# A rarely taken branch in a routed-expert kernel: its DMAs on GpSimd, its skipping arm next to the branch, no prefetch marks

## The chip, the cores and the metric

One core of one Trainium2 chip runs the whole program. The metric is device microseconds of one execution; the kernel before takes 772.91 us (median of three). TensorE (PE in the profile) multiplies matrices, VectorE (DVE), ScalarE (ACT) and GpSimd (POOL) do the rest of the arithmetic, SyncE (SP) issues most DMAs. Each engine runs its own instruction stream and waits on semaphores for the others.

## The reference, cut to what matters

Three layers follow each other: attention within clusters, a mixture of 8 experts in which each token goes to one expert, and a bilinear layer.

```python
# x: (1536, 512), the rows of the attention's output
expert_idx = np.argmax(xn @ en.T / tau, axis=1)      # xn, en: normalised rows
gate_w = probs[np.arange(N), expert_idx]
for e in range(8):
    mask = expert_idx == e                           # how many rows: known at run time
    h = np.maximum(x[mask] @ w1[e], 0.0)             # w1[e]: (512, 1024)
    out[mask] = gate_w[mask, None] * (h @ w2[e])     # w2[e]: (1024, 512)
return ((out @ w_a) * (out @ w_b) @ w_out)           # w_a, w_b: (512, 1536)
```

How many tokens an expert gets is not known when the program is built.

## The kernel before, in words

Up to about 289 us the attention runs, and near its end each token's row is scattered by GpSimd into `xs_d` in DRAM, where every expert has a stretch of its own (L739). Then the experts take their turns in order of their size. `WIDTHS` (L26) gives each turn a fixed number of rows, 256 to 160, which the program computes whether or not the expert has so many. A loop over G (L1433) steps through 8 turns of 8 slices of the hidden layer; slice G's first product is in `layer1(G)`, its second two steps later in `layer2(G - LAG)`, and at the end of a turn `ys_e` holds the results, which `put_rows` (L1305) writes to `ys_d` by a DMA of SyncE.

An expert with more rows than its turn's width is "crowded". `limits()` (L1059) computes on VectorE the largest surplus, `most`. At G == 5 (`GR`) `rare()` (L1172) is called: every engine loads `most` into a register (L1174) and branches (L1175). Where it is above zero, the body computes the surplus rows of each expert in a loop of 128 rows at a time, with the expert's weights loaded anew. For the inputs that are timed `most` is zero, so every engine skips the body; the loops in it do not run. A skipping arm of its own stands for the body in each engine's stream: it adds to every semaphore what the body would have added, so that later waits find the same counts. Before it adds to a semaphore it waits until all that was counted on it earlier has arrived. A DMA that SyncE issues counts on one of eight rings' semaphores, which it shares with ScalarE's DMAs; DMAs that GpSimd issues count on eight others.

Weights come by SyncE. The experts' weights of most turns are loaded into four `raw` buffers of 512 KB (`load_raw`, L156) and split by ScalarE (L207) and VectorE (L208) into a high and a low part in the tiles `w`; a raw buffer is free again when VectorE has read it. The turns of widths 160 and 176 take theirs unsplit, by `load_whole` (L180), which at G == 5 issues four loads right behind the branch. `load_xe` (L1134) loads a turn's rows from `xs_d` by a DMA of ScalarE's queue into one of two buffers, which it shares with the tiles `ys_e`; so the third turn's load waits until `ys_0` has been written out, and what stands behind it in ScalarE's stream waits with it. The order of all this is written out by hand: each engine works through its stream in program order.

Before the change three engines have a mark for the branch (`mark_branch_hint_location`), which names the arm that is likely and becomes a prefetch instruction in that engine's stream: TensorE (L1173), VectorE (L1453) and SyncE (L1488).

Of the kernel before, what the change touches and what calls it, by code (L numbers as in the profile page):

```python
# [22 lines left out]
P = 128  # L23
# [8 lines left out]
GR = 5  # L32
# [16 lines left out]
def kernel(  # L49
# [15 lines left out]
    nc = tc.nc  # L65
# [5 lines left out]
    NTOK = B * S  # L71
# [10 lines left out]
    RX = NTOK + P  # L82
# [14 lines left out]
    xs_d = dram.tile([NE * RX, DM], F32, name="xs_d")  # L97
    ys_d = dram.tile([DM, NTOK + CAP], F32, name="ys_d")
    ys_v = ys_d.rearrange("(j p) n -> p j n", p=P)
# [3 lines left out]
    chunks = []  # L103
# [78 lines left out]
    def skip_whole():  # L182
        while nsplit[0] // 4 in whole:
            nsplit[0] += 4
            ndone[0] += 4
# [671 lines left out]
    for s in range(nst):  # L857
        g_, h, t = steps[s]
        pp = g_[0]
        i = s % SPP  # L860
# [206 lines left out]
    def further():  # L1067

        nc.vector.tensor_tensor(out=prod, in0=col(turn_c), in1=row(turn_c), op=ALU.is_gt)
        summed(obase, prod, row(over))  # L1070
        summed(turn_of, at, row(turn_c))
        nc.vector.tensor_tensor(out=bef, in0=col(turn_of), in1=row(turn_of), op=ALU.is_gt)
        summed(pbase, bef, row(held))
        nc.vector.tensor_reduce(out=key[:, 0, 0:1], in_=over.rearrange("p o e -> p (o e)"), axis=AX.X, op=ALU.add)
        nc.vector.tensor_tensor(out=pbase, in0=pbase, in1=key[:, :, 0:1].to_broadcast([P, 1, NE]), op=ALU.add)
        nc.vector.tensor_copy(ov_i[:, :NE], obase[0:1, 0, :])
        nc.vector.tensor_tensor(out=prod[0:1], in0=at[0:1].rearrange("p e q -> p q e"), in1=pbase[0:1].to_broadcast([1, NE, NE]), op=ALU.mult)
        with nc.allow_low_precision(reason="whole numbers below 2^24"):
            nc.vector.tensor_reduce(out=ov_i[:, NE:2 * NE], in_=prod[0:1], axis=AX.X, op=ALU.add)
            nc.vector.tensor_tensor(out=ov_s, in0=over[0:1].rearrange("p o e -> p e o").to_broadcast([1, NE, OVM]),  # L1080
                                    in1=ovt.rearrange("p (o j) -> p o j", o=1).to_broadcast([1, NE, OVM]), op=ALU.is_gt)
            nc.vector.tensor_reduce(out=ov_i[:, 2 * NE:3 * NE], in_=ov_s, axis=AX.X, op=ALU.add)
            nc.vector.tensor_tensor(out=ov_i[:, 3 * NE:], in0=ebase[0:1, 0, :], in1=cap[0:1, 0, :], op=ALU.add)
        nc.vector.tensor_copy(cnt_i, cnt[0:1, :, 0])
# [85 lines left out]


    def rare():  # L1172
        tc.mark_branch_hint_location("rare", "LikelyTaken", engines=[mybir.EngineType.PE])  # L1173
        n_most = nc.values_load(most, min_val=0, max_val=NTOK)  # L1174
        with tc.If(n_most > 0, label="rare"):  # L1175
            further()
            ovw = [big.tile([P, 2, 4, 512], F32, tag=f"w{NSLOT - 1 - c}", name=f"ov_w{c}") for c in range(2)]
            ovb_ = big.tile([P, 8, 512], F32, tag=f"w{NSLOT - 3}", name="ov_b")
            xr, yr = ovb_[:, 0, :], ovb_[:, 1, :]
            xrT = ovb_[:, 2, :].rearrange("p (j t) -> p j t", t=P)  # L1180
            hT = ovb_[:, 3:5, :].rearrange("p a (j t) -> p (a j) t", t=P)

            ph = ps_s.tile([P, 4, P], F32, tag=f"sc{CT}", name="ov_ph")
            py = ps_s.tile([P, DM], F32, tag=f"sc{CT + 1}", name="ov_py")
            pt = py.rearrange("p (j t) -> p j t", t=P)
            nc.vector.memset(yr, 0.0)
            n_t = [nc.values_load(cnt_i[0:1, e:e + 1], min_val=0, max_val=NTOK) for e in range(NE)]
            for e in range(NE):
                i = nc.sync.dma_start(out=xs_d[bass.ds(n_t[e] + e * RX, P), :], in_=yr)
                if e == 0:  # L1190
                    for o in scatters:
                        tc.add_manual_dep(i.ins, o.name, DATA, reason="rows of every scatter")
            for e in range(NE):
                n_e = nc.values_load(ov_i[0:1, 2 * NE + e:2 * NE + e + 1], min_val=0, max_val=OVM)
                row = nc.values_load(ov_i[0:1, e:e + 1], min_val=0, max_val=NTOK)
                first = nc.values_load(ov_i[0:1, 3 * NE + e:3 * NE + e + 1], min_val=e * RX, max_val=e * RX + CAP)
                with tc.For_i(0, n_e, 1) as it:
                    nc.sync.dma_start(out=xr, in_=xs_d[bass.ds(nc.s_assert_within(first + it * P, min_val=e * RX, max_val=e * RX + NTOK), P), :])
                    for c in range(FF // 512):
                        for z in range(2):  # L1200
                            nc.sync.dma_start(out=ovw[c][:, z], in_=chunks[4 * e + 2 * c + z])
                    for j in range(DC):
                        nc.tensor.transpose(pt[:, j, :], xr[:, j * P:(j + 1) * P], ident)
                    nc.vector.tensor_copy(xrT, pt)
                    for c in range(FF // 512):
                        for f in range(4):
                            for j in range(DC):
                                nc.tensor.matmul(ph[:, f, :], ovw[c][:, 0, j, f * P:(f + 1) * P], xrT[:, j, :], start=(j == 0), stop=(j == DC - 1))
                        nc.vector.tensor_scalar(out=hT[:, 4 * c:4 * c + 4, :], in0=ph, scalar1=0.0, scalar2=None, op0=ALU.max)
                    for c in range(FF // 512):  # L1210
                        for f in range(4):
                            for j in range(DC):
                                nc.tensor.matmul(pt[:, j, :], ovw[c][:, 1, f, j * P:(j + 1) * P], hT[:, 4 * c + f, :],
                                                 start=(c == 0 and f == 0 and j == 0), stop=(c == FF // 512 - 1 and f == 3 and j == DC - 1))
                    nc.vector.tensor_copy(yr, py)
                    nc.sync.dma_start(out=ys_v[:, :, bass.ds(nc.s_assert_within(row + it * P, min_val=0, max_val=NTOK), P)],
                                      in_=yr.rearrange("p (j t) -> p j t", t=P))


# [119 lines left out]
    def split_x2(ck, u):  # L1339

        hi, lo = xT_t["b", ck, u]
        nc.scalar.copy(hi, lo.bitcast(F32))
        nc.vector.tensor_sub(lo, lo.bitcast(F32), hi)
# [89 lines left out]
    for G in range(total_f + tot + LAG):  # L1433
        I = G - total_f

        skip_whole()
        room = 4 * (NSLOT + 2 * (max(G - LAG, 0) // 4)) - nsplit[0]
        if 4 * NCE <= nsplit[0] and I < 0 and G % NF > 1:
            narrow_a(min(room, 1))
        if G == 1:  # L1440
            ranks()
        if G == 2:
            limits()
        if G == GR:
            rare()
        if I < 0:
            layer1(G)
            if G in (2, NF - 1):
                load_xe(1 if G == 2 else 2)
            if G == NF:  # L1450
                further()
            if G == GR - 2:
                tc.mark_branch_hint_location("rare", "LikelyTaken", engines=[mybir.EngineType.DVE])  # L1453
            e, f = divmod(G, NF)
            if 2 * NF <= G < 3 * NF:
                next(rr, None)
            if G > 3 * NF:
                next(gg, None)
            if f == (5 if e else NF - 2):
                if e + 1 < NE:  # L1460
                    trans_x(e + 1, xe_t[e + 1])
            if f == 5 and 0 < e < NE - 2:
                load_xe(e + 2)
        elif I < tot:
            bil1(I)
            next(pg_, None)
        for ck, u in X2S.get(I, ()):
            split_x2(ck, u)
        if I >= LAG:
            for J in after[I]:  # L1470
                bil2(J)
        elif G >= LAG:
            layer2(G - LAG)
        for ck, u in X2.get(I, ()):
            load_x2(ck, u)
        put_rows(G - LAG)
        if 3 <= G < total_f:
            load_whole(G)
        if nsplit[0] < 4 * NCE:

            ramp = RAMP0 + 2 * min(G, GR - 2) + RAMP * max(G - GR + 1, 0)
            split_some(min(room, 2 * G + lead - nsplit[0], ramp - nsplit[0], 4 * NCE - nsplit[0]))
        elif I < 0:
            narrow_c()
            narrow_b(1)
            narrow_d()
        if G == GR - 1:
            tc.mark_branch_hint_location("rare", "LikelyTaken", engines=[mybir.EngineType.SP])  # L1488


# [28 lines left out]
```

## Time and profile before

| | us |
|---|---|
| median of three runs | 772.91 |
| lowest and highest | 771.47, 772.96 |
| the profiled execution's own time | 772.48 |
| its span, first to last instruction | 770.4 |
| TensorE busy | 749.1 |
| VectorE, ScalarE, GpSimd busy | 465.4, 374.2, 106.0 |

The span is what the profile shows; the own time is what the measurement of the same execution gives, and 2.1 us lie around the span. A busy time is a mean over stages: the branch lies at 300 to 317 us, at the start of the expert layer. In the views "engine name with q" is that engine's queue of instructions (register loads, branches, semaphores, DMA issues), which do not count as busy.

### The profile page before, as it was taken

How to read it: one execution, taken by the hardware profiler on the slowest of the kernel's cores; microseconds unless marked ns; L12 is line 12 of the kernel's file. 1: busy time of each engine (PE TensorE's matmuls, PEld its weight loads, DVE VectorE, ACT ScalarE, POOL GpSimd, SP SyncE). 2: the span in 40 equal slices, each digit the busy share in tenths (PEclk: the TensorE clock that was granted, in tenths of full speed). 3: DMA queues.
4: the chain of work that ended last, by engine and by line, in shares of the span. 5: the costliest groups of instructions: out<-in, count | busy, mean ns of one | idle time of the engine just before them, and what ended most of it. 6: DMA issues, size and time to landing. Idle time of an engine off the chain costs nothing.

```text
span 770.4 us, 12666 instructions
## 1 busy us (share of the span) xinstructions
PE 749.1 (97%) x4777; PEld 629.4 (82%) x4777; DVE 465.4 (60%) x911; ACT 374.2 (49%) x769; POOL 106.0 (14%) x145
## 2 busy tenths in 40 slices
PE   8989999999999998999999999999999999999996
PEld 5667777767777668999999999888898888888996
DVE  7877676787767666477876799686653121121211
ACT  5666766678666674366655555344323121111211
POOL 6303203052200040000000003222001020000201
PEclk9999999999999999999999999999999999999999
DMA  6327223163121036789879877464411010000100
GB/s 187 85 85 266 48 76 85 59 199 100 46 48 32 28 110 202 275 310 294 274 235 255 284 229 235 113 138 112 134 29 55 1 55 1 1 0 1 55 1 28
DMA packets 48132, 91.87 MB, mean 119 GB/s; under 512 B 6328, under 2 KB 20280, under 8 KB 48064
## 3 DMA queue, kind: packets, MB, share of 16 engines
q1 hardware_dynamic: 43856, 81.01, 34.9%
q0 software_dynamic: 2304, 6.31, 2.1%
q10 hardware_dynamic: 1904, 3.67, 1.4%
q8 instruction: 39, 0.64, 0.3%
q14 instruction: 29, 0.24, 0.1%
HBM read 69.27 MB, written 14.04 MB: 108 GB/s over the span
## 4 chain that ended last, share of the span: by engine, by line
issue 28%; PE 23%; DMA 4%; DVE 2%; POOL 1%; ACT 1%; SPq 0%; POOLq 0%; ACTq 0%; DVEq 0%
PE ab L1169 7%; PE y L1286 4%; PE y L1290 2%; PE h L1250 2%; DMA raw<-in_moe_w_dram 2%; PE h L1169 2%; PE h L1242 2%; PE o_sc L1414 1%; DMA ys_d<-ys 1%; PE y L1291 1%; PE h L1251 1%; POOL out_dram L1392 1%; DVE w L208 1%; ACT w L207 1%; PE o_pp L1414 1%
## 5 line engine op out<-in xcount | busy, mean ns | idle before, releaser
L1373 DVE TENSOR_TENSOR ga<-ab,ga 128x256 f32<-128x256 f32 (+1 forms) x48 | 26.7, 557 | 156.8 <-PE ab L1169 111.0
L1169 PE MATMUL ab<-xT_b,w 128*128 128x256 f32 (+1 forms) x720 | 113.2, 305 | 0.0
L606 ACT ACTIVATE E<-sc,nmx 128x768 f32<-128x768 f32 x96 | 86.7, 903 | 54.0 <-DVE nmx L601 42.1
L1169 PE MATMUL ab<-x,w 128*128 128x512 f32 x432 | 108.1, 390 | 0.0
L1169 PEld LDWEIGHTS ab<-xT_b,w 128*128 128x128 f32 x720 | 98.6, 190 | 7.2
L601 DVE TENSOR_REDUCE nmx<-sc 128x1 f32<-128x768 f32 x96 | 91.4, 953 | 7.6 <-PE sc L593 6.5
L1169 PEld LDWEIGHTS ab<-x,w 128*128 128x128 f32 x432 | 81.1, 188 | 17.2
L621 PEld LDWEIGHTS et<-ident,E 128*128 128x128 f32 x576 | 62.3, 140 | 34.6 <-ACT ET L625 14.4
L621 PE MATMUL et<-ident,E 128*128 128x128 f32 x576 | 82.3, 279 | 4.2 <-ACT E L606 1.7
L627 DVE COPY ET<-et 128x384 f32<-128x384 f32 x96 | 52.6, 548 | 53.7 <-PE et L621 50.8
L1372 ACT COPY ga<-ab 128x256 f32<-128x256 f32 (+1 forms) x48 | 23.0, 480 | 126.9 <-PE ab L1169 123.8
L592 PE MATMUL sc<-K,Q 80*128 80x512 f32 x192 | 72.9, 380 | 1.4 <-DMA Q<-ohT 1.1
L648 PE MATMUL pv<-ET,v 128*64 128x384 f32 (+2 forms) x408 | 73.0, 479 | 0.6 <-ACT ET L625 0.5
L208 DVE TENSOR_TENSOR w<-raw,w 128x1024 fp32r<-128x1024 f32 x48 | 58.1, 1219 | 21.1 <-ACT w L207 20.5
L1414 PE MATMUL o_sc<-w,g 128*128 128x512 f32 x288 | 69.5, 390 | 0.0
L1374 ACT CAST g<-ga 128x256 fp32r<-128x256 f32 (+1 forms) x48 | 24.7, 514 | 84.1 <-DVE ga L1373 84.1
L1414 PEld LDWEIGHTS o_sc<-w,g 128*128 128x128 f32 x288 | 53.9, 188 | 11.3
L593 PE MATMUL sc<-K,Q 128*128 128x512 f32 x192 | 61.2, 340 | 0.0
L1286 PE MATMUL y<-hh,w 128*128 128x256 f32 (+3 forms) x416 | 59.3, 290 | 0.0
L207 ACT CAST w<-raw 128x1024 fp32r<-128x1024 f32 x48 | 50.3, 1049 | 18.5 <-DMA raw<-in_moe_w_dram 11.7
L1286 PEld LDWEIGHTS y<-hh,w 128*128 128x128 f32 x416 | 54.4, 190 | 0.3 <-DVE ys L1260 0.3
L625 ACT COPY ET<-et 128x384 f32<-128x384 f32 x96 | 45.6, 475 | 2.6 <-PE et L621 2.6
(268 smaller groups left out, 1204.0 us busy)
## 6 DMA issues: line engine op xcount, KB each, us to landing
raw<-in_moe_w_dram SPq DMA_DIRECT2D x48, 512.0 KB
w<-in_moe_w_dram SPq DMA_DIRECT2D x16, 512.0 KB
raw<-in_moe_w_a_dram SPq DMA_DIRECT2D x12, 512.0 KB
raw<-in_moe_w_b_dram SPq DMA_DIRECT2D x12, 512.0 KB
raw<-in_moe_w_out_dram SPq DMA_DIRECT2D x12, 512.0 KB
xs_d<-zero SPq DMA_DIRECT2D x8, 512.0 KB
xe<-xs_d ACTq DMA_DIRECT2D x7, 512.0 KB
v<-in_v_dram SPq DMA_DIRECT2D x8, 384.0 KB
```

The source lines that it names most:

```text
L207: nc.scalar.copy(hi, w)
L208: nc.vector.tensor_sub(lo, w, hi)
L592: nc.tensor.matmul(ps[:, lo:hi], Q3[:, qs], K3[:, h * S + lo:h * S + hi], start=True, stop=False)
L593: nc.tensor.matmul(ps[:, lo:hi], Q2[:, qs], K2[:, h * S + lo:h * S + hi], start=False, stop=True)
L601: nc.vector.tensor_reduce(out=nmx[pp][:, h, t:t + 1], in_=sc[s], axis=AX.X, op=ALU.max, negate=True)
L606: nc.scalar.activation(e, sc.pop(s), AF.Exp, bias=nmx[pp][:, h, t:t + 1], accum_out=sums[pp][:, t, h:h + 1])
L621: nc.tensor.transpose(pt[:, j * P:(j + 1) * P], e[:, kt * P:(kt + 1) * P], ident)
L627: nc.vector.tensor_copy(dst, src)
L648: nc.tensor.matmul(pv[h * D:(h + 1) * D, :], vt[:, h, kt, :], ets[g, h][:, kt, :n * P], start=(kt == 0), stop=(kt == NT - 1))
L1169: nc.tensor.matmul(ps, s_, m_, start=(i == 0), stop=(i == len(ops) - 1))
L1286: nc.tensor.matmul(ys_ps[e][j // 2][:, j % 2, :wd], w[:, m_, ff, j * P:(j + 1) * P], s_, start=(f == 0 and i == 0 and j % 2 == 0), stop=(l ...
L1414: nc.tensor.matmul(o_ps[ck][t], s_[:, t * P:(t + 1) * P], w_[:, m_], start=(f == 0 and i == 0), stop=(J == I and f == NF2 - 1 and i == 2))
```

## The change

The DMAs in the body are issued by GpSimd instead of SyncE; the branch asks that its false arm, which skips, comes next in the stream; the three marks go. The body is otherwise the same, and the timed inputs still skip it.

```diff
     def rare():
-        tc.mark_branch_hint_location("rare", "LikelyTaken", engines=[mybir.EngineType.PE])
         n_most = nc.values_load(most, min_val=0, max_val=NTOK)
-        with tc.If(n_most > 0, label="rare"):
+        with tc.If(n_most > 0, label="rare", preferred_fallthrough_block=False):
             further()
...
             for e in range(NE):
-                i = nc.sync.dma_start(out=xs_d[bass.ds(n_t[e] + e * RX, P), :], in_=yr)
+                i = nc.gpsimd.dma_start(out=xs_d[bass.ds(n_t[e] + e * RX, P), :], in_=yr)
...
                 with tc.For_i(0, n_e, 1) as it:
-                    nc.sync.dma_start(out=xr, in_=xs_d[...])
+                    nc.gpsimd.dma_start(out=xr, in_=xs_d[...])
                     for c in range(FF // 512):
                         for z in range(2):
-                            nc.sync.dma_start(out=ovw[c][:, z], in_=chunks[4 * e + 2 * c + z])
+                            nc.gpsimd.dma_start(out=ovw[c][:, z], in_=chunks[4 * e + 2 * c + z])
...
-                    nc.sync.dma_start(out=ys_v[...],
+                    nc.gpsimd.dma_start(out=ys_v[...],
                                       in_=yr.rearrange("p (j t) -> p j t", t=P))
...
-            if G == GR - 2:
-                tc.mark_branch_hint_location("rare", "LikelyTaken", engines=[mybir.EngineType.DVE])
...
-        if G == GR - 1:
-            tc.mark_branch_hint_location("rare", "LikelyTaken", engines=[mybir.EngineType.SP])
```

## Rows read from the trace of the kernel before

**Rows 1.** The page's engine table: busy us, share of the span, instructions.
```profile
PE 749.1 (97%) x4777; PEld 629.4 (82%) x4777; DVE 465.4 (60%) x911; ACT 374.2 (49%) x769; POOL 106.0 (14%) x145
```

**Rows 2.** TensorE's timeline: start, us, operation, in brackets the idle time before.
```profile
304.55 1.67 PE L1169 MATMUL h<-xT,w 128*128 128x256 f32 x12 [0.30 <-PEq L1175]
...
342.14 1.70 PE L1169 MATMUL h<-xT,w 128*128 128x256 f32 x12 [1.36 <-DVE hh L1247]
...
354.92 1.70 PE L1169 MATMUL h<-xT,w 128*128 128x256 f32 x12 [0.40 <-DVE hh L1247]
...
367.03 0.47 PE L1290 MATMUL y<-hh,w 128*128 128x448 f32 x1 [1.06 <-DVE ys L1299]
```

**Rows 3.** The branch's line: ns (min/median/max), first and last start in us.
```profile
L1175 SPq EVENT_SEMAPHORE  x9: 17/17/17, 311.4 to 316.3; - x9
L1175 PEldq EVENT_SEMAPHORE  x2: 51/51/51, 304.3 to 304.4; - x2
L1175 DVEq EVENT_SEMAPHORE  x2: 21/21/21, 304.5 to 304.6; - x2
L1175 POOLq COMPARE_BRANCH  x1: 53/53/53, 300.2 to 300.2; - x1
L1175 PEldq COMPARE_BRANCH  x1: 397/397/397, 302.6 to 302.6; - x1
...
L1175 DVEq COMPARE_BRANCH  x1: 84/84/84, 303.9 to 303.9; - x1
...
L1175 POOLq EVENT_SEMAPHORE  x1: 17/17/17, 304.6 to 304.6; - x1
L1175 SPq COMPARE_BRANCH  x1: 70/70/70, 307.4 to 307.4; - x1
```

**Rows 4.** Waits of SyncE's queue, 300 to 320 us: total us, times, longest.
```profile
SPq L1175 <- SPq L1175: 8.4, 4, 4.0
```

**Rows 5.** The DMA view, 300 to 320 us in 40 equal slices: rate.
```profile
GB/s 205 168 385 406 430 369 209 352 377 234 66 131 172 234 324 328 344 344 373 397 385 401 393 430 307 250 172 127 78 25 25 12 0 0 4 168 295 266 406 393
```

**Rows 6.** SyncE's timeline behind the branch.
```profile
316.83 2.20 SPq L180 DMA_DIRECT2D w<-in_moe_w_dram  x4
...
320.54 0.42 SPq L1310 DMA_DIRECT2D ys_d<-ys  x1
```

**Rows 7.** The chain that ended last, in order of time: start, us, what.
```profile
320.54 9.47 DMA ys_d<-ys
...
334.52 4.91 DMA raw<-in_moe_w_dram
```

**Rows 8.** ScalarE's timeline behind the branch.
```profile
327.26 1.07 ACT L1159 CAST xT<-xT 128x512 fp32r<-128x512 f32 x2
...
330.61 1.04 ACT L207 CAST w<-raw 128x1024 fp32r<-128x1024 f32 x1 [2.27 <-DMA ys_d<-ys]
```

**Rows 9.** Who waited for whom, GpSimd: total us, times, longest.
```profile
POOL tab_d L994 <- DVE id_gate L987: 113.9, 1, 113.9
```

**Rows 10.** Busy us by window; the last three columns: granted clock, DMA share, GB/s.
```profile
320.00:340.00 20.00, 20.00 (x157) 20.00 (x157) 11.56 (x14) 11.56 (x18) 0.00 (x0) 1.00 0.96 336
```

**Rows 11.** The page's DMA queues that fetch instructions: packets, MB, share of 16 engines.
```profile
q8 instruction: 39, 0.64, 0.3%
q14 instruction: 29, 0.24, 0.1%
```

**Rows 12.** The windows at the end of the span, with the granted clock.
```profile
766.00:768.00 2.00, 0.00 (x0) 0.00 (x0) 0.00 (x0) 0.00 (x0) 0.35 (x2) 0.92 0.43 168
768.00:770.00 2.00, 0.00 (x0) 0.00 (x0) 0.00 (x0) 0.00 (x0) 0.00 (x0) 0.50 0.00 0
```

**Rows 13.** TensorE's timeline at the start and at the end of the span.
```profile
1.21 4.02 PE L263 MATMUL wps<-ones 128*128 128x512 bf16 x9 [1.21 <-DVE ones L247]
...
6.55 0.83 PE L263 MATMUL wps<-ones 128*128 128x512 bf16 x3
...
762.78 1.52 PE L1414 MATMUL o_pv<-w,g 128*128 128x512 f32 x6
```

More of the change, by code (lines that the diff above doesn't have):

```diff
@@ L1197, in rare @@
                 with tc.For_i(0, n_e, 1) as it:
-                    nc.sync.dma_start(out=xr, in_=xs_d[bass.ds(nc.s_assert_within(first + it * P, min_val=e * RX, max_val=e * RX + NTOK), P), :])
+                    nc.gpsimd.dma_start(out=xr, in_=xs_d[bass.ds(nc.s_assert_within(first + it * P, min_val=e * RX, max_val=e * RX + NTOK), P), :])
                     for c in range(FF // 512):
                         for z in range(2):
-                            nc.sync.dma_start(out=ovw[c][:, z], in_=chunks[4 * e + 2 * c + z])
+                            nc.gpsimd.dma_start(out=ovw[c][:, z], in_=chunks[4 * e + 2 * c + z])
                     for j in range(DC):
@@ L1215, in rare @@
                     nc.vector.tensor_copy(yr, py)
-                    nc.sync.dma_start(out=ys_v[:, :, bass.ds(nc.s_assert_within(row + it * P, min_val=0, max_val=NTOK), P)],
+                    nc.gpsimd.dma_start(out=ys_v[:, :, bass.ds(nc.s_assert_within(row + it * P, min_val=0, max_val=NTOK), P)],
                                       in_=yr.rearrange("p (j t) -> p j t", t=P))
```

## The prediction, made before the changed kernel was run

> **What bounds the kernel now.** I read the page first, its table of engines: TensorE is busy 749.1 of 770.4 us [rows 1]. What the change can gain is therefore bounded by TensorE's idle time behind the branch, and what it can lose by any hole that it makes there. So the second view was TensorE's timeline with the idle time ahead of each piece [rows 2]. From the branch to 445 us there are four holes: 0.30 us at the branch itself, then 1.36 us at 342.14, 0.40 us at 354.92 and 1.06 us at 367.03, 3.12 us together and 2.82 without the first. The third view was the two lines of the branch [rows 3], where the reader is to look, engine by engine, at the time from the compare to the first semaphore of the skipping arm: GpSimd 300.2 + 0.05 to 304.6 (4.35 us), SyncE 307.4 + 0.07 to 311.4 (3.9 us), VectorE 303.9 + 0.08 to 304.5 (0.5 us), TensorE 302.6 + 0.4 to 304.3, which is only when its own last matmul had ended. The waits of SyncE's queue give the same line 8.4 us in four waits, the longest 4.0 [rows 4]: the first is the jump, the other three are the arm's semaphores, each waiting until one ring of earlier loads has landed. The DMA view of that stretch shows what this costs [rows 5]: from 313 to 317.5 us (places 27 to 35 of the 40) the rate falls from about 390 to some 50 GB/s, so 4.5 us x 0.34 MB/us = 1.5 MB, three loads of 512 KB, are not moved.
>
> Last SyncE's timeline [rows 6], the chain that ended last [rows 7] and ScalarE's timeline [rows 8]. Behind the arm SyncE issues four weight loads from 316.83 on, a raw load, and at 320.54 the write of `ys_0`, which lands 9.47 us later, behind those five. The next `xe` load needs that tile's buffer and stands in ScalarE's queue ahead of the weight split of L207, which starts at 330.61 after 2.27 us of idling for that write; from there the ring raw load, L207, L208, next raw load runs late and opens the three later holes.
>
> **The change part by part.** *DMAs to GpSimd.* Of SyncE's nine semaphores in the skipping arm the eight of its DMA rings go to GpSimd's arm; SyncE keeps the one of its register loads. SyncE is free some 5 us earlier for this alone (311.4 instead of 316.3). GpSimd's rings last carried the scatters, all issued ahead of its own compare at 300.2, and GpSimd then waits 113.9 us for `id_gate` [rows 9], so nine short semaphores there cost nothing. If that cover were gone they would cost up to the 5 us that SyncE's took. Who waits for them now are the first weight loads and the `xe` load behind the arm; GpSimd has done them before SyncE reaches its compare at 307.4. What then follows: the five loads are issued from 312 or 308 instead of 316.83, while the loads issued earlier are still under way (the last lands at 316.3, when SyncE passes its last semaphore), so the hole in the DMA closes; at the 336 GB/s of the stretch behind [rows 10] one load takes 1.56 us, so the five have landed by 316.3 + 5 x 1.56 = 324.1 and `ys_0`, issued when it is computed (about 320), by 325 at the latest. ScalarE reaches the `xe` load at 328.3 (end of the casts of L1159, 327.26 + 1.07): its 2.27 us are gone, and nothing is late in their place. Carried along the ring this takes back 2.27 of the 2.82 us of later holes; at the most all of it. ScalarE's `xe` load just behind the branch also stops waiting for SyncE; TensorE waits for neither, so that is worth nothing.
>
> *The arm behind the branch, and no marks.* Where things stand now is read from rows 3: the time is lost ahead of the semaphores and none after them (SyncE's last at 316.3, its next DMA at 316.83; TensorE's last at 304.4, its next matmul at 304.55 [rows 2, 6]). So today the body of the rare path lies behind the branch, then the skipping arm, then the rest of the kernel. The flag swaps the two arms. Nothing in the diff moves the rest, which both arms must reach, so I take the order to become: arm, body, rest. Then the skip isn't free of its jump. The jump only stands behind the semaphores instead of ahead of them, and nothing marks it for prefetch any more.
>
> For SyncE and GpSimd that changes little: they paid 3.9 and 4.35 us with the old order (SyncE with a mark) and pay it again; SyncE's loads start at about 312. VectorE, now unmarked, may lose 4 us from 304.6 on; its next work waits for TensorE's matmuls, which come later still: nothing.
>
> TensorE is the one that pays. Its arm can't start its semaphores before its last matmul has ended (304.25), and the jump comes after them, at about 304.55, with an empty array. The body has 8 experts x 68 matmuls, each with a weight load: 1,088 instructions. One queue fetches code in 39 pages of 0.64 MB / 39 = 16 KB [rows 11]; I take it for TensorE's, whose 2 x 4777 matmuls and weight loads [rows 1] are 245 a page, while the other engines have far fewer; the jump is then over 4.4 pages. Its price isn't in the trace: the bounds are 0.5 us (VectorE's, target there) and 5.5 us (GpSimd's 4.35 and one more microsecond for a page twice the size). I take 4.6: GpSimd's and SyncE's mean of 4.1, and 0.5 for the page, since 0.3% of 16 engines' 770 us over 39 pages is 0.95 us each against 0.1% over 29, 0.42 us, for the others [rows 11].
>
> The Trainium skill ("Runtime: NRT & Kernel Launch", section "Instruction fetch mechanics") speaks against the change in the same way: a taken branch to a page outside the two-page window has to fetch it before going on. The 3.9 and 4.35 us of rows 3 agree; by this rule an order without a jump would cost TensorE nothing and the one that I assume would cost it a fetch.
>
> A hole of almost 5 us touches the clock. At the end of the kernel the last matmul ends at 764.30 and the granted clock is at half (1.2 GHz) from 767.7, worked out from 0.92 in 766:768 and 0.50 behind [rows 12, 13]. At the start the nine warming matmuls from 1.21 take 4.02 us, 0.42 us apart, where three later ones fit into 0.83 [rows 13]: at least 4 us at half rate. So a fall would cost 0 (it doesn't come) to 2.6 us; I take 1.5.
>
> **The sum**, against the profiled execution (772.48 us, span 770.4; the median of the three others is 772.91, the lowest 771.47, so it stands in their middle): 772.48 + 4.6 (jump) + 1.5 (clock) - 2.6 (later holes; between 2.27 and 2.82, since the delay gives the loads more lead) = 776.0 us.
>
> **The rivals.** *No jump is left.* If the rest of the kernel lies directly behind the arm and the body is put elsewhere, no engine jumps: SyncE's loads start at 307.6, TensorE keeps its 0.3 us hole (it waits for its own matmuls), and only the gain is left: 772.48 - 2.3 = 770.2, at most 769.3 with 2.82 and the first hole gone. For it: the flag is meant to say what comes next. Against it: today's order has arm and rest side by side with the body in front, and a swap of the two arms is all the diff asks for. The point that decides is TensorE's first matmul behind its semaphores: at 304.6 here, near 309 in the forecast.
>
> *The jump is cheap.* The same order, but TensorE pays 3.5 us or less and the clock stays up, against 2.8 us given back: 773.2. For it: the clock's fall at the end came 3.4 us after the last matmul, close to such a hole. Against: the two engines that jump to code that isn't there pay more with smaller pages.
>
> *Nothing moves.* The DMAs' move does nothing for TensorE because the ring of raw loads sets the later holes by itself, and no jump is left: 772.5. Against: ScalarE's 2.27 us stand in that chain.
>
> **How the numbers follow.** Jump as forecast 0.55 (own range 773.8 to 778); no jump 0.3 (769.3 to 771.2); cheap jump 0.1; nothing moves 0.05. The measurement tells 0.2% (1.5 us) from no change. Slower: 0.53, the forecast but for its lowest end. Faster: 0.29, all but the upper edge of the second. Same: 0.18, the two last and those edges. The range from 769.9 to 777.8 reaches over the other side's case; it leaves out its lowest part and a clock that stays low longer than at the start.
>
> **What would show it.** In the changed profile: SyncE's arm has one semaphore and its queue's waits at L1175 lose the three on rings (if not, the first part is wrong); the DMA rate has no hole at 313 to 317; ScalarE's 2.27 us wait for `ys_0` is gone; TensorE has a hole of 4 to 5.5 us right behind its semaphores, with the granted clock below 1 behind it. A hole of 0.3 us there and 770 us makes the forecast wrong at the step "the rest stays behind the body"; a hole of 4.6 us with the later holes as before makes the gain wrong.

## The result and the profile after

The changed kernel takes 778.09 us (median of five runs, 777.54 to 780.89) against 771.47 us for the kernel before (five runs, 770.31 to 772.96): a ratio of 1.0094, 95% interval 1.0074 to 1.0114 (the two medians alone give 1.0086). It is slower by 0.9%. The forecast was 776.0 us with a range up to 777.8, so the sign and the mechanism came out and the size did not: the time lies 0.3 us above the range, and the change costs some 7 us where 3.5 were forecast.

The profiled execution of the changed kernel took 780.70 us with a span of 779.2 us. First the engine table of its page, and its two queues that fetch instructions [rows 1, 11]:

```profile
PE 751.3 (96%) x4777; PEld 631.4 (81%) x4777; DVE 465.5 (60%) x911; ACT 373.9 (48%) x769; POOL 106.2 (14%) x145
...
q8 instruction: 40, 0.66, 0.4%
q14 instruction: 32, 0.26, 0.1%
```

The same 4777 matmuls are busy for 2.2 us longer, which is already a hint at the clock. The branch's line is L1174 now (one line was removed ahead of it). ns are min/median/max, then the first and the last start; where a group has two, the second COMPARE_BRANCH is the jump at the end of the arm [rows 3]:

```profile
L1174 POOLq EVENT_SEMAPHORE  x5: 17/43/43, 299.8 to 300.1; - x5
...
L1174 PEldq COMPARE_BRANCH  x2: 95/4021/7947, 302.0 to 304.0; - x2
...
L1174 PEldq EVENT_SEMAPHORE  x2: 51/51/51, 303.7 to 303.9; - x2
L1174 SPq COMPARE_BRANCH  x2: 41/47/53, 306.6 to 306.8; - x2
L1174 POOLq INC_SWDGE_SEM  x1: 412/412/412, 300.2 to 300.2; - x1
...
L1174 SPq EVENT_SEMAPHORE  x1: 17/17/17, 306.7 to 306.7; - x1
```

The reader is to see three things. On every engine the semaphores now start right behind the compare (TensorE's once its last product has ended, at 303.7), so the arm does lie behind the branch. Each engine shows two COMPARE_BRANCH where it had one, so a jump is left, behind the arm. TensorE's lasts 7.95 us, from 304.0 to 312.0. SyncE's shows as 0.04 us, but its next instruction starts only at 313.0, of which more further down. SyncE has one semaphore left of nine; GpSimd's take 0.8 us and nobody waits for them.

TensorE's timeline, with the idle time ahead of a piece in brackets [rows 2]:

```profile
302.09 1.60 PE L1285 MATMUL y<-hh,w 128*128 128x256 f32 x12
312.03 2.93 PE L1169 MATMUL h<-xT,w 128*128 128x256 f32 x12 [8.34 <-issue]
314.76 2.60 PE L1285 MATMUL y<-hh,w 128*128 128x256 f32 x12
317.19 1.60 PE L1169 MATMUL h<-xT,w 128*128 128x256 f32 x12
...
348.34 1.70 PE L1169 MATMUL h<-xT,w 128*128 128x256 f32 x12 [0.71 <-DVE hh L1246]
...
375.92 0.47 PE L1289 MATMUL y<-hh,w 128*128 128x448 f32 x1 [1.17 <-DVE ys L1298]
```

and the windows over it (the last three columns are the granted clock, the DMA share and GB/s):

```profile
304.00:306.00 2.00, 0.00 (x0) 0.00 (x0) 0.00 (x0) 0.00 (x0) 0.00 (x0) 1.00 0.67 225
306.00:308.00 2.00, 0.00 (x0) 0.00 (x0) 0.00 (x0) 0.00 (x0) 0.00 (x0) 0.69 1.06 323
308.00:310.00 2.00, 0.00 (x0) 0.00 (x0) 0.00 (x0) 0.00 (x0) 0.00 (x0) 0.50 1.02 358
...
314.00:316.00 2.00, 2.00 (x11) 2.00 (x11) 0.42 (x1) 1.00 (x2) 0.00 (x0) 0.50 0.04 13
316.00:318.00 2.00, 2.00 (x15) 2.00 (x14) 1.23 (x1) 0.31 (x1) 0.00 (x0) 0.75 0.52 189
318.00:320.00 2.00, 2.00 (x21) 2.00 (x20) 0.76 (x2) 0.81 (x2) 0.00 (x0) 1.00 0.98 353
```

From 304 to 312 no engine computes at all. In that hole the granted clock falls to 0.50 (1.2 GHz), and most of the next 24 matmuls run at it, until about 317 (the window 316 to 318 is at 0.75): from 312.03 to 317.19 they take 5.16 us, where the two pieces behind the jump took 2.95 before (the first starts at 304.55, and the third at 307.50 in the same timeline). That is 2.2 us, the same 2.2 by which TensorE's busy time grew.

The bill of the two profiled executions, 779.2 - 770.4 = 8.8 us of span: 8.04 for the jump (8.34 - 0.30), 2.2 for the clock, less 0.94 for the two later holes (0.71 + 1.17 against 2.82), less 0.56 because TensorE reached the branch earlier (303.69 against 304.25). The sum is 8.74. Around the span lie 1.5 us against 2.1, so the own times differ by 8.2. That is no chance: the time around the span is about 1.5 us (1.43 to 1.54) in every execution of every kernel with the body's DMAs on GpSimd, and about 2.1 (2.02 to 2.15) in those of the kernel before.

The five runs of the changed kernel lie at 777.5 to 778.1 and at 780.7 to 780.9; the profiled one belongs to the upper, some 2.6 us above the median.

### The profile page after: what moved, and what is told of

The parts are those of the page before. It is cut to its first block, busy times and chain, and to the rows that moved or that the text cites. A ratio compares the mean times of both kernels' runs of the same rounds, so it can differ in the third digit from the quotient of the medians.

```text
span 779.2 us, 12681 instructions
## 1 busy us (share of the span) xinstructions
PE 751.3 (96%) x4777; PEld 631.4 (81%) x4777; DVE 465.5 (60%) x911; ACT 373.9 (48%) x769; POOL 106.2 (14%) x145
## 4 chain that ended last, share of the span: by engine, by line
issue 29%; PE 24%; DMA 3%; DVE 3%; POOL 1%; ACT 1%; POOLq 0%; SPq 0%; DVEq 0%; ACTq 0%
PE ab L1169 6%; PE y L1285 4%; DMA raw<-in_moe_w_dram 2%; PE y L1289 2%; PE h L1249 2%; PE h L1169 2%; PE h L1241 2%; PE o_sc L1413 1%; DVE w L208 1%; PE y L1290 1%; PE h L1250 1%; POOL out_dram L1391 1%; PE o_pp L1413 1%; PE o_pv L1413 1%; ACT w L207 1%
## 5 line engine op out<-in xcount | busy, mean ns | idle before, releaser
L1169 PE MATMUL h<-xT,w 128*128 128x256 f32 (+1 forms) x288 | 40.0, 289 | 11.0 <-issue 8.3
```

Of the source, the lines that this page charges most:

```text
L1169: nc.tensor.matmul(ps, s_, m_, start=(i == 0), stop=(i == len(ops) - 1))
```

## The experiments

Twelve runs were made, of nine further kernels and three repetitions. Theory: TensorE's jump lands on code that has not been fetched, and the array stands still meanwhile. The rivals: the time goes into GpSimd's DMAs and semaphores, or into SyncE's late loads.

### The DMAs alone, and the order alone

`e1_pool_only` is the kernel before with the first part of the change; `e2_order_only` is the changed kernel with that part undone:

```diff
 e1, in the kernel before (the same at all four places):
-                i = nc.sync.dma_start(out=xs_d[...], in_=yr)
+                i = nc.gpsimd.dma_start(out=xs_d[...], in_=yr)
 e2, in the changed kernel:
-                i = nc.gpsimd.dma_start(out=xs_d[...], in_=yr)
+                i = nc.sync.dma_start(out=xs_d[...], in_=yr)
```

> The kernel before with one part of the change: the body's DMAs on GpSimd; old order of the arms, all three marks kept. My theory (the loss is TensorE's jump behind its skipping arm, the gain is SyncE's arm without waits on the rings): TensorE keeps its 0.3 us hole at the branch, SyncE's queue loses the three waits on rings, the 2.27 us wait of ScalarE for ys_0 goes, and 1 to 2.8 us of the later holes with it: 0.9964 to 0.9987 of before. Rival (GpSimd's part of the arm costs something itself, or what waits for GpSimd's rings now is late): 1.002 or more, with a hole at TensorE that ends on GpSimd. Rival (the ring of raw loads sets the later holes by itself): 0.999 to 1.001.

Measured: 770.42 us, ratio 0.9974 (0.9958 to 0.9989), faster than the kernel before. `e8_pool_again` repeated it:

> e1_pool_only once more, for a second ratio against the kernel before (the first was 0.9974, 0.9958 to 0.9989), and beside e7_pool_quiet on the same chip: 0.996 to 0.999.

769.51 us, ratio 0.9977 (0.9964 to 0.9990). In the profile of `e1_pool_only`, first the waits of SyncE's queue, 300 to 320 us [rows 4]:

```profile
SPq L1175 <- SPq L1175: 3.8, 1, 3.8
```

then the DMA rate over the same 20 us in 40 slices [rows 5]:

```profile
GB/s 258 188 373 385 434 365 184 279 369 324 352 340 299 262 332 320 299 315 393 373 389 389 430 336 221 201 205 352 299 287 352 389 254 258 360 373 352 397 410 385
```

then the timelines of SyncE and of ScalarE [rows 6, 8]:

```profile
311.65 2.57 SPq L180 DMA_DIRECT2D w<-in_moe_w_dram  x4
...
320.00 0.41 SPq L1310 DMA_DIRECT2D ys_d<-ys  x1
```

```profile
327.25 1.07 ACT L1159 CAST xT<-xT 128x512 fp32r<-128x512 f32 x2
...
328.83 1.04 ACT L207 CAST w<-raw 128x1024 fp32r<-128x1024 f32 x1 [0.50 <-ACT xT L1159]
```

and TensorE's later holes:

```profile
353.57 1.69 PE L1169 MATMUL h<-xT,w 128*128 128x256 f32 x12 [0.68 <-DVE hh L1247]
...
365.44 0.47 PE L1290 MATMUL y<-hh,w 128*128 128x448 f32 x1 [0.80 <-DVE ys L1299]
```

This is the chain of the prediction, link by link: SyncE's wait shrinks from 8.4 us to the jump's 3.8, its loads start 5.2 us earlier, the rate no longer breaks down from 313 to 317, the weight split starts at 328.83 in place of 330.61, and the later holes shrink from 2.82 to 1.48 us. In the second run's profile no hole above 0.1 us is left between the branch and 445 us. The first part is worth 0.25%, some 2 us. Of these 0.6 us lie outside the span (about 1.5 us around it in all 24 executions of the two runs, against about 2.1 in the kernel before): the prediction had no term for them, and no view shows what they are.

> The changed kernel with the body's DMAs back on SyncE: skipping arm next to the branch, no marks. My theory: TensorE jumps behind its arm as in the changed kernel, hole of 5 to 8.5 us and half clock behind it; SyncE's arm waits for its rings again: 1.007 to 1.013 of before. Rival (the DMAs' move makes the long fetch, since GpSimd now has a larger body to jump over and fetches at the same time): hole of 4.6 us or less, 1.002 to 1.005.

Measured: 778.65 us, ratio 1.0083 (1.0060 to 1.0106). The branch's line and TensorE's timeline in its profile:

```profile
L1174 SPq EVENT_SEMAPHORE  x9: 17/17/17, 306.6 to 314.3; - x9
...
L1174 PEldq COMPARE_BRANCH  x2: 95/3322/6550, 302.3 to 304.3; - x2
```

```profile
310.95 2.93 PE L1169 MATMUL h<-xT,w 128*128 128x256 f32 x12 [6.95 <-issue]
...
373.28 0.47 PE L1289 MATMUL y<-hh,w 128*128 128x448 f32 x1 [0.73 <-DVE ys L1298]
```

The whole loss stands in the order and the marks; the rival with GpSimd's DMAs falls. The rival with SyncE's late loads falls too: here they start at 317.40, in `e5_quiet` (below) at 309.04, and both kernels lose the same 0.8%. And although SyncE's nine semaphores last until 314.3 here, the later holes shrink all the same, to 0.73 us: TensorE comes 6.4 us late (310.95 against 304.55), and, as far as these profiles show, that gives the loads the lead which the DMAs' move gives in e1. So the gain does not come on top of the loss: e1 and e2 add up to +0.57%, and both together cost 0.94%; each ratio is uncertain by some 0.2%, so the difference is only just outside that.

### The marks alone

`e3_no_marks` is the changed kernel without the flag: old order, DMAs on GpSimd, no marks.

```diff
-        with tc.If(n_most > 0, label="rare", preferred_fallthrough_block=False):
+        with tc.If(n_most > 0, label="rare"):
```

> The changed kernel with the old order of the arms: DMAs on GpSimd, no marks, the arm behind the body. My theory (what counts is that TensorE jumps to code that nothing has fetched, wherever the jump stands): TensorE's compare at about 302.5 jumps, its last matmuls cover 1.3 us, so the hole is 1.3 us shorter than in the changed kernel, 4 to 7 us, and the clock may still fall: 1.004 to 1.010 of before. Rival (it is the order, the jump behind the semaphores, that costs): hole of 0.3 to 0.5 us as before and 0.996 to 1.000.

Measured: 775.87 us, ratio 1.0038 (1.0024 to 1.0053). Its repetition, `e11_no_marks_again`:

> e3_no_marks once more (old order, DMAs on GpSimd, no marks). TensorE's jump took 5.31 us there. If the order of the jumps sets that, it is 5.0 to 5.6 again, with TensorE's page ahead of ScalarE's and VectorE's; if it was chance, up to 8. Time 775 to 776.5, ratio 1.002 to 1.006.

775.70 us, ratio 1.0042 (1.0026 to 1.0059). The jump of TensorE in e3 and what follows it:

```profile
L1174 PEldq COMPARE_BRANCH  x1: 5312/5312/5312, 303.5 to 303.5; - x1
```

```profile
303.60 1.60 PE L1285 MATMUL y<-hh,w 128*128 128x256 f32 x12
309.13 2.90 PE L1169 MATMUL h<-xT,w 128*128 128x256 f32 x12 [3.93 <-PEq L1174]
```

In e11 the jump took 5.19 us and the hole was 3.81; both holes lie just under the 4 to 7 us expected for e3. With the old order the jump stands ahead of the semaphores, so it begins while the last product still runs and 1.7 us of it are covered. Against e1, where only the marks differ, the lost marks cost 1.0038 - 0.9974 = 0.64%, some 5 us, and it is TensorE whose hole grows, from 0.30 to 3.93 us, with another 2.5 us for the slow clock behind it. The swap of the arms costs the rest, 1.0094 - 1.0038 = 0.56%, some 4 us. The three marks were taken out together, and the swapped order was never run with marks: what one mark is worth alone, and whether one would bring the code behind the swapped arm in time, is not shown.

### How far the jump goes

`e4_short_body`, `e6_half_body` and `e9_five_body` are the changed kernel with the body's loop cut short:

```diff
-            for e in range(NE):
+            for e in range(1):      # e4; 4 in e6, 5 in e9
```

> The changed kernel with a body for the first expert alone (the surplus of the other seven is left out; the timed inputs have none): TensorE's code in the body falls from 1,088 matmuls and weight loads to 136, less than one page of 245. My theory: the same jump goes to code that is there or comes next; hole of 0.3 to 1 us, full clock, and the gain of the DMAs' move is seen alone: 0.996 to 0.999 of before. Rival (the jump or the arm costs by itself, whatever it jumps over): hole of 5 us or more and 1.006 or more.

> The changed kernel with a body for four experts in place of eight (the surplus of the other four is left out): TensorE's jump is over 544 instructions in place of 1,088, over two pages in place of four. Theory 'any target that is not yet fetched costs one fetch, however far': jump 6 to 8 us, hole 6 to 8, time 777 to 780 as with eight. Rival 'the price grows with the distance': between the run with one expert (0.31 us, 771.0) and eight, a jump of about 3 to 4 us and 773.5 to 775.

> The changed kernel with a body for five experts (the surplus of three is left out). With four, TensorE stalled a second time, for 2.53 us, two matmuls behind the jump's target. Theory 'the target lay at the end of its 16 KB page': one expert more moves the target by 136 instructions, about half a page, so the second stall goes, one hole of 6.5 to 8.5 us stays, and the time falls from 782.9 to 777.5 to 780 although the jump is longer. Rival 'a body of this size costs two stalls': both stalls stay and 782 to 784.

| experts in the body | matmuls and weight loads jumped over | jump, us | TensorE's hole, us | time, us | ratio |
|---|---|---|---|---|---|
| 1 (e4) | 136 | 0.31 | 0.71 | 771.00 | 0.9986 (0.9971 to 1.0002) |
| 4 (e6) | 544 | 7.01 | 7.41 + 2.53 | 782.92 | 1.0147 (1.0126 to 1.0167) |
| 5 (e9) | 680 | 6.77 | 7.17 | 779.64 | 1.0099 (1.0070 to 1.0129) |
| 8 (changed) | 1,088 | 7.95, 6.75 | 8.34, 7.15 | 778.09, 779.02 | 1.0094, 1.0095 |

TensorE behind the jump with one, with four and with five experts:

```profile
304.39 1.70 PE L1169 MATMUL h<-xT,w 128*128 128x256 f32 x12 [0.71 <-PEq L1174]
```

```profile
311.01 0.79 PE L1169 MATMUL h<-xT,w 128*128 128x256 f32 x2 [7.41 <-issue]
314.33 2.30 PE L1169 MATMUL h<-xT,w 128*128 128x256 f32 x10 [2.53 <-issue]
```

```profile
312.31 2.93 PE L1169 MATMUL h<-xT,w 128*128 128x256 f32 x12 [7.17 <-issue]
```

With one expert the arm and its jump stay and the loss is gone: not the arm costs, but the distance. From 544 instructions on the price does not grow with it, so a price for each page jumped over is refuted; it fits one fetch for a target that is not there, as at all three distances tried. With four experts two matmuls run and TensorE stands still a second time, from 311.80 to 314.33, and a second 16 KB transfer of its code lies in that stall, from 311.86 to 313.21. With it e6's time, 782.92 us, came out above what either theory expected. That the target lay at the end of its page, so that the next page had to come too, was the reason given for e9, and there the second stall is gone, as expected, although the jump is longer. The Trainium skill ("Runtime: NRT & Kernel Launch", section "Instruction fetch mechanics") says that a jump out of the pages at hand must wait for a fetch; the 0.31 us against 6.77 us and more agree with it.

### Why the fetch takes 5 to 8 us

Left was the size: SyncE and GpSimd paid 3.9 and 4.35 us in the kernel before [rows 3]. `e0_after_again` is the changed kernel once more:

> The changed kernel once more, for a second sample of TensorE's jump behind its arm. Its five earlier executions had spans of 776.1 to 779.4 us, and the profiled one, with a jump of 7.95 us, was among the long ones (779.2). If the length of the jump is what differs between executions, a profile with a span near 776.4 shows a jump shorter by 2 to 2.8 us, near 5.5, and a hole of about 5.5 to 6; if the difference lies elsewhere, the jump is again near 7.9. Median 777.5 to 780.

It ran 779.02 us, ratio 1.0095 (1.0076 to 1.0114), with a jump of 6.75 us. Its profiled execution took 779.90 us, so the jump in an execution of 777.3 to 778.2 us was not seen, and the expectation could not be tested. Two edits then aimed at the jump. `e5_quiet` issues early weight loads behind the branch; `e10_pe_first` lets ScalarE and VectorE, which jump shortly before TensorE, jump after it:

```diff
 e5, the bound in load_whole:
-        ... 2 * G + 40, 4 * NCE if G >= GR else 4 * (NSLOT - 3)):
+        ... 2 * G + 40, 4 * NCE if G >= GR else 0):
 e10, ahead of the branch:
     def rare():
+        scr = left.tile([P, 2, 16], F32, name="scr")
+        for _ in range(16):
+            nc.scalar.copy(scr[:, 0, :], ident[:, :16])
+            nc.vector.tensor_copy(scr[:, 1, :], ident[:, :16])
```

> The changed kernel, with the unsplit weight loads that it issues ahead of the branch issued behind it, so that the DMA engines have less to do while TensorE's jump waits for its page. Theory 'the page stands behind the weight loads on the DMA engines': the jump falls from 6.5 to 7.9 us to 5 us or less, the hole to about 5, and the time to about 775. Rival 'the price is the jump's own': jump and hole stay at 6.5 to 8 and the time at 777.5 to 780. If the DMA share from 304 to 310 us is still near 1 in the profile, the run tells nothing of the two.

> The changed kernel with sixteen small copies ahead of the branch on ScalarE and on VectorE, which are idle there, so that both reach their branch and their jump some 3 us later, after TensorE's jump at about 304 us. So far the jump took 6.5 to 7.95 us where ScalarE and VectorE had jumped just before and the DMA share was near 1, and 5.3 us (e3_no_marks) where TensorE jumped first at the same share. Theory 'the fetches stand in line behind one another': the jump falls to 5.0 to 5.6 us with the DMA share from 304 to 308 still above 0.8, hole about 5.5, time about 775 to 776.5. Rival 'only the weight loads delay it': jump 6.5 to 8 us and 777.5 to 780.

The jump in e5 and its windows:

```profile
L1174 PEldq COMPARE_BRANCH  x2: 95/2652/5210, 301.9 to 303.9; - x2
```

```profile
304.00:306.00 2.00, 0.00 (x0) 0.00 (x0) 0.00 (x0) 0.00 (x0) 0.00 (x0) 1.00 0.70 227
306.00:308.00 2.00, 0.00 (x0) 0.00 (x0) 0.00 (x0) 0.00 (x0) 0.00 (x0) 0.55 0.26 84
```

The same in e10, with the engines that now come later:

```profile
L1178 PEldq COMPARE_BRANCH  x2: 95/2842/5590, 302.1 to 304.2; - x2
...
L1178 ACTq COMPARE_BRANCH  x2: 38/44/49, 306.6 to 306.8; - x2
L1178 DVEq COMPARE_BRANCH  x2: 51/53/55, 307.0 to 307.3; - x2
```

```profile
304.00:306.00 2.00, 0.00 (x0) 0.00 (x0) 1.66 (x10) 1.73 (x9) 0.00 (x0) 1.00 0.82 285
306.00:308.00 2.00, 0.00 (x0) 0.00 (x0) 0.43 (x3) 0.41 (x2) 0.00 (x0) 0.77 1.00 375
```

In the trace the 16 KB transfer of the fetch stands with its own start, so a jump splits in two: from the jump to that transfer, and from there to the end of the jump.

| kernel | ScalarE and VectorE jump | jump, us | to the transfer | from it | DMA share in the wait | 8 KB transfers in the wait |
|---|---|---|---|---|---|---|
| changed | before TensorE | 7.95 | 5.5 | 2.5 | 0.90 | 3 |
| changed again | before | 6.75 | 4.0 | 2.8 | 0.93 | 3 |
| e2 | before | 6.55 | 4.0 | 2.5 | 0.95 | 2 |
| e5, fewer loads | before (SyncE too) | 5.21 | 2.5 | 2.7 | 0.75 | 4 |
| e10 | after | 5.59 | 3.0 | 2.6 | 0.88 | 1 |
| e3 | after | 5.31 | 2.8 | 2.5 | 0.87 | 1 |
| e11 | after | 5.19 | 2.8 | 2.4 | 0.92 | 1 |

The wait is the time from the jump to the start of the transfer. The last column counts the 8 KB packets that start in it on q14, the other queue that fetches instructions; the 16 KB ones of q8 were taken for TensorE's, and one of them starts inside each of these jumps.

The second part hardly moves, 2.4 to 2.8 us; all the spread is in the wait ahead of the transfer. It is shorter by 1 to 3 us if fewer loads run, and also, at nearly the same DMA share, if TensorE jumps ahead of the other engines. "Only the weight loads delay it" is thus refuted as the only cause, and so is "the price is the jump's own": as far as these single executions show, both the loads and the other engines' fetches lengthen it. In time little came of it: e5 777.23 us, ratio 1.0081 (1.0063 to 1.0098), and e10 777.31 us, 1.0068 (1.0047 to 1.0090), both above what was expected, and e5's jump too stays just above its 5 us; e10's profile has later holes of 0.51 and 1.78 us. Their intervals overlap those of the changed kernel, so what is shown is the shorter jump, each in one execution, and not a shorter time.

### A version that beats both

`e7_pool_quiet` joins e1 and the edit of e5, to have SyncE jump earlier:

> The kernel before with two edits: the body's DMAs on GpSimd (as in e1_pool_only) and the early unsplit weight loads issued behind the branch (as in e5_quiet); marks and old order stay. If SyncE's jump, like TensorE's, is shorter when the DMA engines have less to do and starts earlier (303.5 in place of 307 us), its loads start near 307.5 in place of 311.7 us, ys_0 is written no later, and the time is at or below that of e1_pool_only: 769 to 770.5. If the four loads moved behind the branch push ys_0's write and the next raw load back, the later holes return: 771 to 773.

770.90 us, ratio 0.9984 (0.9968 to 0.9999), between the two expected ranges. SyncE's jump falls to 0.5 us, from 3.8 in e1, and its loads start earlier, by 5.0 us in the two profiles:

```profile
SPq L1175 <- SPq L1175: 0.5, 1, 0.5
```

```profile
306.66 5.96 SPq L180 DMA_DIRECT2D w<-in_moe_w_dram  x8
```

But there are eight to issue now, and the write of the results of the first turn comes at 321.06 in place of 320.00; counted from TensorE's first product behind the branch, which is 1.05 us later in this profile, both are 15.5 us. It is no better than e1. The kernel to keep is `e1_pool_only`: 0.9974 and 0.9977 against the kernel before, which itself beats the changed one.

## Why the prediction was wrong

*Which term failed.* "Its price isn't in the trace: the bounds are 0.5 us ... and 5.5 us", and 4.6 was taken. The jump's hole was 8.04 us longer in the profiled execution, 6.85 in the second one and 6.65 in e2: 2 to 3.4 us over the value taken, and over the upper bound each time. The bound was built from GpSimd's and SyncE's stalls and one microsecond for a larger page. The size of the page was the wrong place to look. In the changed kernel TensorE jumps at 304, as the third engine within 1.2 us (ScalarE's jump starts at 302.8, VectorE's at 303.6) and behind four weight loads issued from 302.34 on. That these loads lie there could be read beforehand, in SyncE's timeline of the kernel before,

```profile
302.88 2.15 SPq L180 DMA_DIRECT2D w<-in_moe_w_dram  x4
```

and in the 324 to 430 GB/s from 307 to 312 [rows 5]; it was read for the loads alone. What the runs showed in place of the 4.6: from the start of the page's transfer on the jump costs 2.4 to 2.8 us, but ahead of it the transfer waits 4.0 to 5.5 us when TensorE jumps behind other engines and weight loads.

*The clock.* 1.5 us was taken out of 0 to 2.6; how the 2.6 was found is not said. Measured: 2.2, by two views that agree (24 matmuls late by 2.2, TensorE busy 2.2 longer). Counted in the same way, to the end of the third group of 12 matmuls, they are late by 2.7 in the second profile of the changed kernel, over that bound, and by 1.35 in e9, whose hole is as long (7.17 us against 7.15).

*What is given back.* 2.6 us was taken, "between 2.27 and 2.82". In the profiled execution it was 0.94; in the second one 2.0 (one later hole, 0.79). The mechanism is right where TensorE is on time (e1, e8). Beside a late TensorE it is not the DMAs' move that gives it back, as e2 shows, and the claim that the hole in the DMA at 313 to 317 closes was wrong there. The rate in the changed kernel [rows 5], SyncE's first instructions behind its branch, and the loads that they issue:

```profile
GB/s 168 385 406 422 357 205 389 365 205 168 233 295 344 348 336 262 262 365 397 410 369 381 377 270 188 147 111 41 25 12 0 16 0 139 258 360 324 393 414 283
```

```profile
L180 SPq FUSED_REGOPS  x4: 46/48/51, 313.0 to 317.1; - x4
```

```profile
315.37 2.27 SPq L180 DMA_DIRECT2D w<-in_moe_w_dram  x4
```

The hole stands where it stood, 312 to 317, because SyncE's own jump was priced too low as well. "[T]hey paid 3.9 and 4.35 us with the old order ... and pay it again" was the term, and the loads were to start at about 312. SyncE jumps at 306.82, now without its mark, and does nothing until 313.0: 6.1 us. Its loads start at 315.37, after another pause of 1.8 us (313.2 to 315.0) whose cause is not shown. In e3 and e11, old order without marks, its jump took 5.9 and 6.2 us, with the mark in e1 and e8 3.8 and 4.0; in e4, where its way is short too, its loads start at 307.20.

*With the measured sizes* the sum is 772.48 + 8.04 + 2.2 - 0.94 - 0.56 - 0.6 = 780.6, against 780.70. In the sum as predicted the jump and the clock were too small (4.1 us) and the gain too large (1.7 us), so the three terms err to the same side, by 5.8 us. What takes 1.2 us of this back is in no term of the prediction: TensorE reached the branch 0.56 us earlier, which is chance, and 0.6 us fell away around the span. And that the median of 778.09 comes within 0.3 us of the range is luck: the profiled execution, on which the sum was built, is 4.7 us over the forecast.

*What held.* The order arm, body, rest, and with it the jump behind the semaphores on an empty array; SyncE's one semaphore; GpSimd's semaphores at no cost; the wait of 2.27 us for `ys_0` in ScalarE, which is gone; the clock below 1 behind the hole.

*The rivals.* "No jump is left" was the order assumed wrongly, and it did not happen; e4, whose jump costs next to nothing, shows about what it would have brought: 771.0 us, close to its 770.2. "The jump is cheap" and "nothing moves" are refuted by the 7.95 us.

*Still open.* Why one execution of the changed kernel pays 1.2 us more for the same jump than another, what holds SyncE for the 1.8 us behind its jump, and where the fetches of several engines hold each other up.

## What to carry to other kernels

Before laying an arm next to its branch, count the instructions of the other arm on each engine: what is skipped has to be jumped over once, at the branch or behind the arm, and on the bounding engine the first place, with a mark, while its last products still run, left a hole of 0.30 us here, without the mark one of 3.8 to 3.9, and the second place without a mark one of 5.6 to 8.3. Price such a jump from the moment in which it is made, with the loads and the other engines' jumps around it, not from another engine's jump in a quieter one. And two edits that shorten and lengthen the same chain should be timed apart: one was worth 2 us, and the other hid it.

## What was not expected of the hardware

A jump of TensorE over 544 instructions or more, without a mark, takes 5.2 to 7.95 us, of which 2.4 to 2.8 come behind the start of the transfer that brings the page; over 136 it takes 0.31. Behind the jump over 544, a second transfer of code two matmuls further on went with a second stall of 2.53 us. The marks did not serve all engines alike: TensorE's jump took 0.40 us with them and 5.2 to 5.3 without; SyncE's 3.8 to 4.0 with them and 5.9 to 6.2 without. Only in e7, with fewer loads ahead of it, did SyncE's marked jump fall to 0.5 us.
